# Attention decode step with a gated feed-forward on Trainium2: the first weight load as eight strided transfers

## The chip, the cores and the metric

The kernel runs on one core of a Trainium2 chip. A core has five engines that run their own instruction streams: TensorE (PE, matrix products), VectorE (DVE), ScalarE (ACT), GpSimd (POOL) and SyncE (SP). In this kernel SyncE issues all the transfers between HBM and the on-chip memory SBUF; the transfers themselves are carried out by 16 DMA engines, called movers below. SBUF has 128 partitions; a tile lies across partitions, and a row of a tile is what one partition holds of it.

The metric is the device time of one execution in microseconds (us). Before the change it is 696.29 us, the median of three runs (696.13 to 696.43).

## What is computed

Two branches read the same `x` of shape (2, 1, 640) and are mixed by a gate. Branch A is one decode step of attention with 32 heads over a cache of 4096 keys and values for each of 2 batch rows; branch B is a feed-forward layer with SiLU. All data are float32.

```python
g = sigmoid((x * gate_w).sum(-1, keepdims=True))

q = (x @ wq).reshape(B, Sq, 32, 128).transpose(0, 2, 1, 3)
scores = einsum("bhqd,bhkd->bhqk", q, k_cache) * 128 ** -0.5
o = einsum("bhqk,bhkd->bhqd", softmax(scores), v_cache)
a = o.transpose(0, 2, 1, 3).reshape(B, Sq, 4096) @ wo

b = einsum("bsf,fd->bsd", silu(einsum("bsd,df->bsf", x, w1)), w2)

return g * a + (1 - g) * b
```

The caches are most of the data: `k_cache` and `v_cache` have 134 MB each, `wq` and `wo` 10.5 MB each, `w1` (640 x 1728) and `w2` 4.4 MB each.

## The kernel before

**Tiles.** SBUF holds three large slabs, `a`, `b` and `v`, each 128 partitions of 16384 floats (64 KB a partition, 8.4 MB in all). The attention is cut into 16 items, a group of four heads of one batch row each. The K of an item fills slab `a` or `b` in turn, its V slab `v`. Each item's K is multiplied by the query and summed by VectorE (L666, L676) and GpSimd (L660), ScalarE takes the exponentials (L705), and TensorE multiplies by V (L756).

**The opening.** Before the first K the slabs serve for the weights. `w1`, viewed as 128 rows of 5 x 1728 floats (34,560 bytes a row), goes to columns 4096 to 12735 of slab `v`; `x` and the gate's weights go behind it in the same slab, on partitions 0 to 2. Of `wq`, four fifths go to slab `a` and the last fifth to the first 4096 columns of slab `v`; `w2` goes to slab `b`. SyncE issues these in the order w1, x, gate, wq (slab a), wq (slab v), w2, and none of them waits for another. TensorE then transposes x (L411), forms the gate (L433), multiplies x by wq (L458), spreads the first query (L478), rearranges the queries (L507) and multiplies x by w1 (L527). The feed-forward's second product with w2 is L584. K of item 0 goes to slab `a` after L458 has read wq there, V of item 0 to slab `v` after L527 has read w1.

**The close.** When the last item's V is in line, `wo` follows in seven transfers, the last three of them to slab `b`, and the output product (L607, L624, L637) adds both branches up.

**How the order is made.** The class `Flow` records every operation in program order, with the names that it reads and writes. `Flow.dma` (its issue shows as L68) gives every load its own semaphore; the 16 movers raise it by 16 in all when the load is complete. Names such as `v.3` stand for parts of a slab, and `part("v", 1, 2, 3, 4, 5)` lists the ones that w1 covers. `Flow.plan` goes through the operations and decides what each one waits for: it looks at the operations that it depends on, in a sorted order, and leaves out those that an earlier wait of the same engine already covers. `Flow.run` then writes the instructions, each behind its waits. The short first parts of the streams of ScalarE, VectorE and TensorE are written inside a small loop (`detour`), and TensorE's work for items 0 to 14 is a loop (`repeat`).

Of the kernel before, what the change touches and what calls it, by code (L numbers as in the profile page):

```python
# [16 lines left out]
class Flow:  # L17
# [22 lines left out]
    def op(self, eng, fn, reads=(), writes=(), by=(), signal=None, loop=None, after=(), lower=()):  # L40
        deps = list(after)
        for r in reads:
            if r in self.writer:
                deps.append(self.writer[r])
            if r.startswith("ps_"):
                deps += [d for d in self.readers.get(r, ()) if d.eng != eng]
        for w in writes:
            if w in self.writer:
                deps.append(self.writer[w])
            deps += self.readers.get(w, ())  # L50
        o = Op(eng, fn, deps, by, signal, loop)
        o.dma, o.lower = False, lower
        o.idx = len(self.ops[eng])
        self.ops[eng].append(o)
        self.all.append(o)
        for r in reads:
            self.readers.setdefault(r, []).append(o)
        for w in writes:
            self.writer[w], self.readers[w] = o, []
        return o  # L60
# [2 lines left out]

        return [self.writer[k] for k in keys if k in self.writer] + [o for k in keys for o in self.readers.get(k, ())]

    def dma(self, eng, dst, src, reads=(), writes=(), signal=None, after=()):
        e = self.engines[eng]
        o = self.op(eng, lambda: e.dma_start(dst, src), reads, writes, signal=signal, after=after)  # L68
        o.dma = True
        if signal is None:  # L70
            o.sem = self.sem(f"load_{len(self.all)}")
        return o

    def plan(self):
        seen = {e: {} for e in self.engines}
        for o in self.all:
            know = seen[o.eng]

            def done(d):
                return d in know.get("dma", ()) if d.dma else know.get(d.eng, -1) >= d.idx  # L80

            def learn(d):
                for e, v in d.know.items():
                    if e == "dma":
                        know["dma"] = know.get("dma", frozenset()) | v
                    else:
                        know[e] = max(know.get(e, -1), v)
                if d.dma:
                    know["dma"] = know.get("dma", frozenset()) | {d}
                else:  # L90
                    know[d.eng] = max(know.get(d.eng, -1), d.idx)

            for d in o.by:
                learn(d)
            for d in sorted(o.deps, key=lambda d: -d.idx):
                if (d.eng == o.eng == "PE") or done(d):
                    continue
                assert d.signal is None and o.loop is None, (o.eng, o.idx, d.eng, d.idx)
                o.waits.append(d)
                d.post = True  # L100
                learn(d)
            o.know = dict(know)
        for e, ops in self.ops.items():
            n = 0
            for o in ops:
                o.post = o.post or o.loop is not None
            for o in ops:
                n += o.post and not o.dma
                o.at = n

    def run(self, eng, ops=None):
        e = self.engines[eng]
        for o in self.ops[eng] if ops is None else ops:
            best = {}
            for d in o.waits:
                s, v = (d.sem, 16) if d.dma else (self.own[d.eng], d.at)
                best[s.name] = (s, max(v, best.get(s.name, (s, 0))[1]))
            for s, v in best.values():
                e.wait_ge(s, v)
            self.issue(o)  # L120
# [44 lines left out]
def gated_decode(nc, x, kc, vc, wq, wo, w1, w2, gate, out):  # L165
# [3 lines left out]
    F = w1.shape[1]  # L169
    J = D // P  # L170
    Q = 4
    QP = P // Q
    HQ = H // Q
    C = Q * SK // P
    NG = C // 4
# [10 lines left out]
    W2 = D // 2  # L186
    NP = HQ // 2
    PR = 2 * Q
    FIRST = 5
    LEAD = HB // 2  # L190
    PACED = (NP - 2) * PR
    items = [(hq, b) for hq in range(HQ) for b in range(B)]
    N = len(items)
# [3 lines left out]
    f = Flow(nc)  # L197
    V, S_, T_, G_ = nc.vector, nc.scalar, nc.tensor, nc.gpsimd

    def sb(name, shape, align=32):  # L200
        return nc.alloc_sbuf_tensor(name, shape, F32, align_bytes=align)[tuple([slice(None)] * len(shape))]

    def bank(name):
        return nc.alloc_psum_tensor(name, [P, 512], F32)[:, :]
# [3 lines left out]
    slab = {n: sb(f"slab_{n}", [P, SLAB], 512) for n in "abv"}  # L208

    def part(n, *ks):  # L210
        return [f"{n}.{k}" for k in (ks or range(8))]
# [11 lines left out]
    xz = sb("xz", [P, J, 32])  # L223
# [10 lines left out]
    spaced = sb("spaced", [P, FR, 32])  # L234
    qall = sb("qall", [P, HQ, B, DH])
    qsb = sb("qsb", [P, DH])
# [11 lines left out]
    ps_q, ps_o, ps_v, ps_acc, ps_t, ps_m, ps_0, ps_1 = (bank(f"ps{i}") for i in range(8))  # L248
# [8 lines left out]
    W1_AT = (J - J0) * H * DH  # L257
# [31 lines left out]
    def load_wo(g):  # L289
# [9 lines left out]


    wq_rows = wq.rearrange("(p j) n -> p (j n)", j=J)
    f.dma(
        "SP",
        slab["v"][:, W1_AT : W1_AT + J * F],
        w1.rearrange("(p j) f -> p (j f)", j=J),
        writes=part("v", 1, 2, 3, 4, 5),
    )
    xg = slab["v"][: B + 1, XG_AT : XG_AT + D]
    f.dma("SP", xg[:B], x.rearrange("b s d -> (b s) d"), writes=part("v", 6))
    f.dma("SP", xg[B : B + 1], gate[None, :], writes=part("v", 7))  # L310
# [6 lines left out]
        writes=part("b"),  # L317
# [8 lines left out]
        reads=["ident"],  # L326
        writes=["ident"],
# [8 lines left out]
    for q in range(Q):  # L336
        f.op(
            "DVE",
            lambda q=q: V.memset(fold[q * QP : (q + 1) * QP, :, q, :], 1.0),
            writes=["fold"] if q == 0 else [f"fold{q}"],  # L340
# [5 lines left out]
        reads=["ident"],  # L346
        writes=["sel"],
# [4 lines left out]
        reads=["ident"],  # L352
        writes=["half"],
# [9 lines left out]
        reads=["sel"],  # L363
        writes=["pick"],
# [4 lines left out]
        reads=["sel"],  # L369
        writes=["own"],  # L370
# [4 lines left out]
        reads=["ident"],  # L375
        writes=["side"],
    )
    for q in range(Q):
        f.op(
            "DVE",  # L380
            lambda q=q: V.tensor_copy(
                spread[:, q * QP : (q + 1) * QP], ident[:, 32 * q : 32 * q + 1].to_broadcast([P, QP])
            ),
            reads=["ident"],
            writes=[f"spread{q}"],
# [3 lines left out]
    for e in range(2):  # L389
# [6 lines left out]
            reads=["ident", "join"],  # L396
            writes=["join"],
        )
        for t in (at, at + 32):
# [3 lines left out]
                reads=["ident", "join"],  # L403
                writes=["join"],
# [18 lines left out]
    for b in range(B):  # L423
# [3 lines left out]
            reads=["ps_v", "xz"],  # L427
            writes=[f"gx{b}"],
# [5 lines left out]
        reads=["ones", "gp"],  # L434
        writes=["ps_o"],
# [7 lines left out]
        reads=["g"],  # L443
        writes=["gc"],
# [4 lines left out]
    qr = (ps_0, ps_1)  # L449
    HALF = HQ // 2  # L450

# [52 lines left out]
    for u in range(2):  # L504
# [9 lines left out]
            reads=["ident", f"qall{u}0"],  # L514
            writes=[f"ps_{u}"],
# [17 lines left out]
                )  # L533
        return last

    f.op("PE", mm_hr, reads=part("v", 1, 2, 3, 4, 5) + ["xz"], writes=["ps_v"])


    tv = turned[:, : 32 * FR].rearrange("p (n r) -> p n r", r=32)
# [2 lines left out]
    for e in range(2):  # L542
# [3 lines left out]
            reads=["ps_v"],  # L546
            writes=[f"spaced{e}"],
# [8 lines left out]
        reads=["he", "gc"],  # L556
        writes=["he"],
    )
    for e in range(2):
# [5 lines left out]
            reads=["he", "turned", "half", "seq"],  # L565
            writes=[f"seq{e}"],
# [132 lines left out]
    def weights(i):  # L699
        s = Ss[i % 2]  # L700

        def fn():
            for q in range(Q):
                lo, hi = q * QP, (q + 1) * QP
                last = S_.activation(  # L705
# [137 lines left out]
    for i in range(N + 1):  # L843
        j = i - 1
# [99 lines left out]
```

## Time and profile before

| | before |
|---|---|
| median of 3 runs | 696.29 us |
| lowest and highest | 696.13, 696.43 us |
| the profiled execution | 696.27 us |
| its span, first to last instruction | 694.9 us |
| bytes moved | 298.36 MB |
| mean rate over the span | 429 GB/s |
| VectorE, GpSimd, TensorE busy | 70%, 38%, 31% |

The span is cut into 40 equal slices, and a line of digits gives the busy share of each in tenths (9 is 90% or more); the line GB/s gives what the movers moved in each slice. In lists of instructions the first two numbers are the start and the duration in us; SPq marks SyncE's issuing of a transfer, which takes SyncE a few tenths of a microsecond, while the movement itself follows later. The list of issues gives the size of one transfer in KB of 1024 bytes and the time from issue to landing. In a table by stretches, each row has the stretch, its length, the busy time of PE, PE's weight load, DVE, ACT and POOL with the instructions in brackets, the granted TensorE clock, the busy share of the movers (over 1 where packets are counted to the stretch in which they begin) and GB/s.

### The profile page before, as it was taken

How to read it: one execution, taken by the hardware profiler on the slowest of the kernel's cores; microseconds unless marked ns; L12 is line 12 of the kernel's file. 1: busy time of each engine (PE TensorE's matmuls, PEld its weight loads, DVE VectorE, ACT ScalarE, POOL GpSimd, SP SyncE). 2: the span in 40 equal slices, each digit the busy share in tenths (PEclk: the TensorE clock that was granted, in tenths of full speed). 3: DMA queues.
4: the chain of work that ended last, by engine and by line, in shares of the span. 5: the costliest groups of instructions: out<-in, count | busy, mean ns of one | idle time of the engine just before them, and what ended most of it. 6: DMA issues, size and time to landing. Idle time of an engine off the chain costs nothing. (4 is left out here: it accounts for less than half of the span.)

```text
span 694.9 us, 3683 instructions
## 1 busy us (share of the span) xinstructions
PE 214.9 (31%) x1478; PEld 72.9 (10%) x1478; DVE 488.9 (70%) x263; ACT 41.2 (6%) x153; POOL 266.0 (38%) x26
## 2 busy tenths in 40 slices
PE   1085031151321406050412305060503215060557
PEld 1022010010110101010100101020101001020113
DVE  2001958898989596896959595986959595978901
ACT  0010010101010102010010101010000101010100
POOL 1000808191826090815335170906244260908100
PEclk9998557566665757575575757575665757575779
DMA  9999999999999999999999999999999999999997
GB/s 378 426 439 460 430 427 426 422 464 430 426 430 422 464 430 426 430 422 464 426 430 430 422 453 438 430 430 422 449 441 430 426 426 438 449 430 426 430 415 312
DMA packets 6217, 298.36 MB, mean 429 GB/s; under 512 B 695, under 2 KB 703, under 8 KB 962
## 3 DMA queue, kind: packets, MB, share of 16 engines
q1 hardware_dynamic: 6210, 298.27, 99.2%
q8 instruction: 4, 0.07, 0.0%
q14 instruction: 3, 0.02, 0.0%
HBM read 298.26 MB, written 0.01 MB: 429 GB/s over the span
## 5 line engine op out<-in xcount | busy, mean ns | idle before, releaser
L756 PE MATMUL ps<-slab_v,pz 128*32 128x512 f32 x960 | 134.7, 724 | 336.3 <-PEq L151 336.3
L660 POOL TENSOR_TENSOR slab_a<-slab_a,qsb 128x7680 f32<-128x7680 f32 x8 | 131.5, 16438 | 207.1 <-DMA slab_a<-in_A_k_cache_dram 192.0
L660 POOL TENSOR_TENSOR slab_b<-slab_b,qsb 128x7680 f32<-128x7680 f32 x8 | 131.4, 16424 | 171.5 <-DMA slab_b<-in_A_k_cache_dram 155.5
L676 DVE TENSOR_REDUCE s<-slab_a 128x68 f32<-128x8704 f32 (+1 forms) x16 | 138.2, 8676 | 0.0
L676 DVE TENSOR_REDUCE s<-slab_b 128x68 f32<-128x8704 f32 (+1 forms) x16 | 138.2, 8676 | 0.0
L666 DVE TENSOR_TENSOR slab_b<-slab_b,ps 128x8704 f32<-128x8704 f32 x8 | 73.7, 9218 | 48.9 <-DMA slab_b<-in_A_k_cache_dram 37.6
L666 DVE TENSOR_TENSOR slab_a<-slab_a,ps 128x8704 f32<-128x8704 f32 x8 | 73.7, 9219 | 45.3 <-DMA slab_a<-in_A_k_cache_dram 45.3
L756 PEld LDWEIGHTS ps<-slab_v,pz 128*32 128x32 f32 x960 | 37.0, 130 | 421.6 <-issue 421.6
L705 ACT ACTIVATE pz<-s,nb 32x128 f32<-32x128 f32 x64 | 25.5, 398 | 563.8 <-PE ps L756 390.7
L794 PE MATMUL ps<-osb,pick 128*128 128x512 f32 x32 | 20.4, 724 | 62.8 <-PEq L151 61.8
L778 DVE SCALAR_TENSOR_TENSOR osb<-ps,rg,own 128x512 f32<-128x512 f32 x16 | 12.0, 749 | 22.8 <-PE ps L756 22.4
L808 DVE TENSOR_REDUCE row<-ps 64x128 f32<-64x512 f32 x16 | 10.9, 682 | 23.3 <-PE ps L794 23.3
L545 DVE COPY spaced<-ps 128x224 f32<-128x224 f32 x2 | 0.7, 386 | 32.3 <-PE ps L527 32.3
L478 PE MATMUL ps<-qall,spread 128*128 (+1 forms) x32 | 7.4, 319 | 32.6 <-PEq L151 31.9
L458 PE MATMUL ps<-slab_a,xz 128*32 128x512 f32 x64 | 8.5, 690 | 16.2 <-DMA slab_a<-in_A_wq_dram 16.2
L794 PEld LDWEIGHTS ps<-osb,pick 128*128 128x128 f32 x32 | 5.4, 210 | 76.9 <-issue 75.0
L705 ACT ACTIVATION_READ_ACCUMULATOR pz<-s,nb 32x1 f32 x64 | 11.8, 184 | 0.0
L756 PE MATMUL ps<-slab_a,pz 128*32 128x512 f32 x64 | 9.3, 744 | 8.0 <-DMA slab_a<-in_A_v_cache_dram 8.0
L478 PEld LDWEIGHTS ps<-qall,spread 128*128 128x128 f32 x32 | 6.6, 224 | 42.8 <-issue 41.2
L815 DVE STREAM_TRANSPOSE ps<-row 64x256 f32<-64x256 f32 x16 | 10.3, 643 | 0.6
L584 PE MATMUL ps<-slab_b,seq 128*32 128x320 f32 x54 | 9.4, 506 | 3.0 <-DVE seq L562 3.0
L607 PE MATMUL ps<-slab_v,oP 128*32 128x320 f32 x96 | 9.2, 434 | 0.6 <-DMA slab_v<-in_A_wo_dram 0.5
(70 smaller groups left out, 92.1 us busy)
## 6 DMA issues: line engine op xcount, KB each, us to landing
slab_v<-in_A_wo_dram SPq DMA_DIRECT2D x2, 2560.0 KB, 19.4
slab_v<-in_B_w_dram SPq DMA_DIRECT2D x1, 4320.0 KB, 14.1
slab_b<-in_B_w_dram SPq DMA_DIRECT2D x1, 4320.0 KB, 46.4
slab_v<-in_A_wo_dram SPq DMA_DIRECT2D x2, 1280.0 KB, 26.7
slab_v<-in_A_wq_dram SPq DMA_DIRECT2D x1, 2048.0 KB, 36.7
slab_b<-in_A_wo_dram SPq DMA_DIRECT2D x1, 1600.0 KB, 31.2
slab_b<-in_A_wo_dram SPq DMA_DIRECT2D x1, 640.0 KB, 32.3
slab_b<-in_A_wo_dram SPq DMA_DIRECT2D x1, 320.0 KB, 32.6
```

The lines of the kernel that those rows point to most:

```text
L478: return T_.matmul(ps_q[:, :DH], spread, qall.rearrange("p h b d -> p (h b) d")[:, i, :], start=True, stop=True,)
L584: last = T_.matmul(early[to : to + 32, :], seq[:, k : k + 2, :].rearrange("p k z -> p (k z)"), slab[n][:, k * HD : (k + 1) * HD], start=(k ...
L607: last = T_.matmul(early[to + 32 * n : to + 32 * n + 32, :], oP[:, at : at + 32], slab["v"][:, s_ * D + n * W2 : s_ * D + (n + 1) * W2], s ...
L660: lambda: G_.tensor_mul(k[:, CV:, :], k[:, CV:, :], qsb[:, None, :].to_broadcast([P, C - CV, DH])),
L666: lambda: V.tensor_mul(k[:, :CV, :], k[:, :CV, :], ps_q[:, None, :DH].to_broadcast([P, CV, DH])),
L676: lambda c0=c0, c1=c1: V.reduce_sum(Ss[i % 2][:, c0:c1], k[:, c0:c1, :], axis=AX.X),
L705: last = S_.activation(pz[lo:hi, :, 4 * q : 4 * q + 4], s[lo:hi].rearrange("p (g c) -> p g c", c=4), AF.Exp, bias=nb[lo:hi], scale=SCALE, ...
L756: last = T_.matmul(ps_v[32 * q : 32 * q + 32, :], pz[:, gr, :], v[:, gr, :], start=(gr < 4), stop=(gr >= NG - 4),)
L778: lambda: V.scalar_tensor_tensor(osb, ps_v.rearrange("p (c d) -> p c d", d=DH), rg, own[:, :, None].to_broadcast([P, 4, DH]), op0=ALU.mult ...
L794: lambda *_: T_.matmul(ps_o, pick, osb.rearrange("p c d -> p (c d)"), start=True, stop=True),
L808: lambda: V.reduce_sum(row, ps_o[:64].rearrange("p (c d) -> p d c", d=DH), axis=AX.X),
L815: lambda: V.transpose(oT.rearrange("p n (e i) -> p n e i", e=2), twice),
```

## The change

The w1 load becomes eight loads. Load `r` takes the rows r, r + 8, ..., r + 120 of the view of 128 rows, whole rows of 34,560 bytes, and puts them on the partitions of the same numbers. All eight raise one semaphore, `load_w1`, and the reader, L527, waits for it to reach 16 x 8 = 128. `Flow.dma` gets two arguments for this, the semaphore and the full count, and `Flow.run` waits for that count. The parts `v.1` to `v.5` are no longer named as written by w1; names `w1.0` to `w1.7` stand in their place, and L527 reads both sets. `Flow.plan` sorts the dependences by the place in the whole program (`turn`) instead of the place in their engine's stream (`idx`).

```diff
@@ class Flow
         o.idx = len(self.ops[eng])
+        o.turn = len(self.all)
...
-    def dma(self, eng, dst, src, reads=(), writes=(), signal=None, after=()):
+    def dma(self, eng, dst, src, reads=(), writes=(), signal=None, after=(), sem=None, full=16):
...
         if signal is None:
-            o.sem = self.sem(f"load_{len(self.all)}")
+            o.sem = sem or self.sem(f"load_{len(self.all)}")
+        o.full = full
...
-            for d in sorted(o.deps, key=lambda d: -d.idx):
+            for d in sorted(o.deps, key=lambda d: -d.turn):
...
-                s, v = (d.sem, 16) if d.dma else (self.own[d.eng], d.at)
+                s, v = (d.sem, d.full) if d.dma else (self.own[d.eng], d.at)
@@ gated_decode
+    EACH = 8
...
-    f.dma(
-        "SP",
-        slab["v"][:, W1_AT : W1_AT + J * F],
-        w1.rearrange("(p j) f -> p (j f)", j=J),
-        writes=part("v", 1, 2, 3, 4, 5),
-    )
+    w1_to, w1_from = slab["v"][:, W1_AT : W1_AT + J * F], w1.rearrange("(p j) f -> p (j f)", j=J)
+    h_w1 = f.sem("load_w1")
+    for r in range(EACH):
+        f.dma("SP", w1_to[r::EACH], w1_from[r::EACH], writes=[f"w1.{r}"], sem=h_w1, full=16 * EACH)
...
-    f.op("PE", mm_hr, reads=part("v", 1, 2, 3, 4, 5) + ["xz"], writes=["ps_v"])
+    f.op("PE", mm_hr, reads=part("v", 1, 2, 3, 4, 5) + [f"w1.{r}" for r in range(EACH)] + ["xz"], writes=["ps_v"])
```

In the order of the instructions, SyncE's stream has eight issues of 16 rows in place of the one of 128 rows, ahead of x; fifteen of VectorE's products on K (L666) lose their wait for TensorE and keep those for ScalarE and for the load; the first K issue loses its wait for wq's load and keeps that for TensorE. The other engines' orders are the same. The new `dma` arguments move the line numbers by one or two (L68 is L69, L411 is L412, L458 is L459, L527 is L528).

## The prediction

> **What bounds the kernel now.** I read the page's head first, then the row of its 40 slices and its queue rows.
>
> ```profile
> span 694.9 us, 3683 instructions
> PE 214.9 (31%) x1478; PEld 72.9 (10%) x1478; DVE 488.9 (70%) x263; ACT 41.2 (6%) x153; POOL 266.0 (38%) x26
> ...
> DMA  9999999999999999999999999999999999999997
> GB/s 378 426 439 460 430 427 426 422 464 430 426 430 422 464 430 426 430 422 464 426 430 430 422 453 438 430 430 422 449 441 430 426 426 438 449 430 426 430 415 312
> DMA packets 6217, 298.36 MB, mean 429 GB/s; under 512 B 695, under 2 KB 703, under 8 KB 962
> ...
> q1 hardware_dynamic: 6210, 298.27, 99.2%
> ```
>
> No compute engine is above 70%; the transfers are above 90% in 39 of 40 slices. The rate has no dip after the first slice, so the question is whether the stream ever stands still. A table by stretches of the inner part, and the chain of waits, answer it.
>
> ```profile
> core 0: us, PE busy (x) PEld busy (x) DVE busy (x) ACT busy (x) POOL busy (x), PEclk, DMA share, GB/s
> 17.40:677.60 660.20, 199.16 (x1298) 64.82 (x1298) 483.13 (x231) 39.53 (x151) 262.89 (x16) 0.66 1.00 434
> ```
>
> ```profile
> 656.93 0.33 SPq L68
> ...
> 658.73 31.24 DMA slab_b<-in_A_wo_dram
> 689.97 0.14 issue
> 690.10 2.69 PE ps L637 x64
> ```
>
> From 17.4 to 677.6 us the 16 movers are busy for 1.00 of the time at 434 GB/s, and the chain ends on the last wo transfer, issued 31 us before it lands: it was in line behind others all that time. So the end is the start of the stream, plus 298.27 MB at its rate, plus a tail of some 5 us. A delay of the whole stream at the front comes out one for one at the end, if nothing later runs dry. The front is this (SyncE's issues and the first users on TensorE, from the timeline; the landing of the first weights from the page's list of issues):
>
> ```profile
> 0.74 0.39 SPq L68 DMA_DIRECT2D slab_v<-in_B_w_dram  x1
> 1.19 0.33 SPq L68 DMA_DIRECT2D slab_v<-in_A_x_dram  x1
> 1.57 0.23 SPq L68 DMA_DIRECT2D slab_v<-in_gate_w_dram  x1
> 1.84 0.36 SPq L68 DMA_DIRECT2D slab_a<-in_A_wq_dram  x1
> ...
> 2.77 0.44 SPq L68 DMA_DIRECT2D slab_b<-in_B_w_dram  x1
> ```
>
> ```profile
> slab_v<-in_B_w_dram SPq DMA_DIRECT2D x1, 4320.0 KB, 14.1
> slab_b<-in_B_w_dram SPq DMA_DIRECT2D x1, 4320.0 KB, 46.4
> ```
>
> ```profile
> 14.26 2.33 PE L411 MATMUL ps<-ident,slab_v 3*128 3x3 f32 x10 [14.26 <-DMA slab_v<-in_A_x_dram]
> ...
> 34.16 8.47 PE L458 MATMUL ps<-slab_a,xz 128*32 128x512 f32 x64 [16.18 <-DMA slab_a<-in_A_wq_dram]
> ```
>
> ```profile
> 42.76 0.33 SPq L68 DMA_DIRECT2D slab_a<-in_A_k_cache_dram  x1
> 51.09 0.33 SPq L68 DMA_DIRECT2D slab_v<-in_A_v_cache_dram  x1
> ```
>
> The w1 transfer is issued at 0.74 and lands by 14.84. All six opening transfers are in line by 3.2 us, the last of them (w2) lands at 2.77 + 46.4 = 49.2, and the next one (K of the first item) joins at 42.8: 6.4 us before the line would be empty. That is the smallest margin of the front, and it moves with the stream, since the K issue waits for the product on wq, which itself waits for wq's landing.
>
> **The change part by part.** *Issues.* One w1 issue becomes eight, seven more on SyncE. From one issue's start to the next takes 0.27 to 0.45 us in the rows above, so x, gate, wq and w2 are issued about 7 x 0.45 = 3.2 us later, wq at 5.0 instead of 1.84. The cover is w1's own movement: wq is needed in line only when w1's last rows have gone, past 13 us. One eighth is 0.553 MB, 1.27 us at 434 GB/s, so issues at 0.45 us stay ahead of the movers. Without that cover it would cost the 3.2 us. Cost taken: nothing.
>
> *Completion marks.* The page's 695 packets under 512 B are 16 for each of the 43 transfers over 128 partitions, and 7 for x, gate and the output. Seven more transfers would make 807, and 6322 packets on q1. What a boundary between small transfers costs is seen at the end, where the last wo block goes out in three pieces (issues from the timeline; landings from the list of issues):
>
> ```profile
> 658.73 1.38 SPq L68 DMA_DIRECT2D slab_b<-in_A_wo_dram  x3
> ```
>
> ```profile
> slab_b<-in_A_wo_dram SPq DMA_DIRECT2D x1, 1600.0 KB, 31.2
> slab_b<-in_A_wo_dram SPq DMA_DIRECT2D x1, 640.0 KB, 32.3
> slab_b<-in_A_wo_dram SPq DMA_DIRECT2D x1, 320.0 KB, 32.6
> ```
>
> Three issues in 1.38 us start about 0.47 apart, so the second piece lands 0.47 + 1.1 = 1.57 us after the first and the third 0.47 + 0.3 = 0.77 after the second. At 434 GB/s their bytes alone take 1.51 and 0.76. A boundary costs 0.01 to 0.06 us, seven of them at most 0.4; I take nothing.
>
> *Waits.* TensorE's w1 product (L527) waits for one semaphore at 128 instead of 16. It stands behind the wq product that ran from 34.16 on, 19 us after w1 is there; a w1 that takes twice as long is still hidden. The new sort key of the planner drops a wait for TensorE from 15 of VectorE's key products (L666) and a wait for wq's load from the first K issue; each keeps a wait that comes later anyway (ScalarE's copy of the same query; the product that read wq), so nothing moves. With both I take nothing.
>
> *The front end of the stream.* In half-microsecond stretches of the start:
>
> ```profile
> 1.00:1.50 0.50, 0.00 (x0) 0.00 (x0) 0.00 (x0) 0.00 (x0) 0.30 (x2) 1.00 0.00 0
> 1.50:2.00 0.50, 0.00 (x0) 0.00 (x0) 0.00 (x0) 0.26 (x1) 0.50 (x2) 1.00 2.80 691
> 2.00:2.50 0.50, 0.00 (x0) 0.00 (x0) 0.33 (x3) 0.50 (x1) 0.50 (x2) 1.00 0.89 276
> 2.50:3.00 0.50, 0.00 (x0) 0.00 (x0) 0.36 (x5) 0.50 (x1) 0.50 (x2) 1.00 0.38 138
> 3.00:3.50 0.50, 0.00 (x0) 0.00 (x0) 0.50 (x3) 0.02 (x1) 0.50 (x2) 1.00 0.00 0
> 3.50:4.00 0.50, 0.00 (x0) 0.00 (x0) 0.47 (x5) 0.00 (x0) 0.37 (x1) 1.00 0.97 415
> ```
>
> Packets are counted where they begin, so the first ones begin between 1.5 and 3.0 us, most of them before 2.5, and the next ones near 4.0. A w1 row is 34,560 B; at 434/16 = 27.1 GB/s it takes 1.27 us, so the first row of an early mover takes 0.7 to 0.8 us more than it needs. A first transfer of 16 rows instead of 128 may be set up sooner. It can't begin before its issue has ended, at 1.13: the gain lies between 0 and 0.9 us. I take 0.4, the middle, since no row says when in that gap the set-up ends.
>
> *The pattern of partitions.* This carries the forecast. Before, each transfer of this size covers all 128 partitions; after, the rows in flight at one time are sixteen partitions eight apart, r, r+8, ..., r+120, the same r on all movers. No row of this trace shows a large transfer to fewer than 128 partitions. What the rows do show is a ceiling: 434 GB/s with all movers at 1.00, for wq, K, V and wo alike, thus a limit at the movers or at their ways into SBUF. If the limit is the movers, each has one row and loses nothing: 0 us. If it is the ways, and these are dealt out by low digits of the partition number, a common step of eight sends several rows of one transfer the same way while other ways idle, and the smallest such crowding, two rows for a way, halves the rate: w1 takes 2 x 10.2 (4.424 MB at 434 GB/s) instead of 10.2 us, **+10.2**. Four to a way would be +30.6. Between 0 and 10.2 I take the upper end: every row at the ceiling had whole tiles, none supports that a sixteenth of the partitions, taken at a power-of-two step, still reaches it.
>
> [...]
>
> A little of the doubling is hidden. Now w1's last row lands at 14.84, while x, which is in line behind w1 rows of its own movers, has been read from 14.26 on: movers are some 0.6 us apart. Where two share a way, one that is late leaves it to its partner. I take -0.5.
>
> Sum: 10.2 - 0.5 - 0.4 = 9.3 on the profiled execution's 696.27 (694.9 of span and 1.4 around it; the median is 696.29): **705.6 us**.
>
> **The rivals.**
> *Movers are the limit; nothing is lost.* For it: each transfer still gives each of the 16 movers one whole row, the same bytes. Against it: only the argument above. The gain at the front less the marks, +0.4 to -0.9: 695.4 to 696.7, I say 696.0.
> *Faster.* The front gives all that its stretches allow: 0.9 us for the set-up and the 0.6 us by which movers are apart, since the movers start level: 694.8. For it: the end waits for the last mover. Against it: the first rows already begin within 1.5 us of each other, and what makes a mover late is not shown to be the set-up.
> *Each transfer pays its start in series.* The eight run down one after the other; the 0.8 us that the first row loses at the start is paid seven more times, 696.3 + 5.6 = 701.9. It decides once the movers don't overlap one transfer's end with the next one's start. Against it: the 0.01 to 0.06 us at the wo pieces. [...]
> *Crowding that is half hidden.* The movers of a crowded pair drift apart and use different ways in turn, 696.3 + 5 = 701.3. [...] Against it: all movers begin within about 1.5 us.
> *It does not do what it says.* Sixteen rows fall on fewer than 16 movers, several in a row: then marks are fewer than 807, and with different movers taken by different transfers the time is that of the first rival; its chance is in there.
>
> **How the numbers follow.** Two rows to a way: 0.61, own range 704.3 to 706.8 (skew and front at their bounds, marks 0.4). Half hidden crowding 0.06, starts in series 0.03, fourfold crowding (about 726) 0.01: slower in all, 0.71. Nothing lost 0.24. Faster by more than 0.2% 0.05. I count 0.2%, 1.4 us, as what a measurement can tell from no change. The range, 695.3 to 707.0, takes in all of the likeliest case and the one in which nothing is lost.
>
> **What would show it.** In the page of the changed kernel: under 512 B 807, if all movers take part. The first of the 40 slices falls from 378 to near 190 GB/s if two rows share a way (217 GB/s from about 2.2 us on, over 17.6 us), and stays at 378 or a little more if not. x's matmul (L412 there) starts near 24 instead of 14.26, the wq product near 43 instead of 34.16, the inner rate stays at 434. The forecast is wrong if the first slice holds its rate; if the slice falls and the end does not follow, a later margin took it. If the wq product comes at 38 to 40, it is a start per transfer or a half hidden crowding: with starts in series there are stretches with no packet between the eighths.

## The result and the profile after

The changed kernel takes 707.15 us (median of 5 runs, 707.09 to 707.39); the kernel before, beside it, 696.29 us. The ratio is 1.0156, with a 95% interval of 1.0145 to 1.0167: 10.86 us slower. The prediction said slower, 705.6 us, and a range up to 707.0; the measured time lies 0.15 us above that range.

The head, the slices and the packet counts of the changed kernel's page:

```profile
span 706.0 us, 3689 instructions
...
DMA  9999999999999999999999999999999999999997
GB/s 200 350 424 454 442 416 443 442 420 427 457 423 420 460 427 416 453 438 416 453 434 420 427 457 423 423 460 423 416 460 431 416 453 438 416 434 449 423 414 305
DMA packets 6329, 298.36 MB, mean 423 GB/s; under 512 B 807, under 2 KB 815, under 8 KB 1074
...
q1 hardware_dynamic: 6322, 298.27, 99.2%
```

The bytes are the same and the line of busy digits is that of before, yet the first slice has 200 GB/s instead of 378 and the second 350 instead of 426; from the third on the numbers lie around those of before. So the loss enters while w1 moves, and nothing later takes it back. Here the first slice's busy digit is 9 at 200 GB/s as at 378: it does not tell a mover that works from one that is held up; only the GB/s line shows it. There are 807 small packets, 112 more, so each of the eight transfers has 16 completion marks: all movers take part.

The stretch from 4 to 22 us, all of it w1, from the table by stretches of the changed kernel:

```profile
4.00:22.00 18.00, 0.00 (x0) 0.00 (x0) 1.42 (x12) 0.00 (x0) 0.00 (x0) 1.00 1.01 212
```

212 GB/s is 0.49 of the 434 GB/s of the inner part before. The front in the timeline of the changed kernel, first SyncE's issues, then TensorE's first users:

```profile
0.74 6.58 SPq L69 DMA_DIRECT2D slab_v<-in_B_w_dram  x8
7.36 0.48 SPq L69 DMA_DIRECT2D slab_v<-in_A_x_dram  x1
7.90 0.23 SPq L69 DMA_DIRECT2D slab_v<-in_gate_w_dram  x1
8.17 0.36 SPq L69 DMA_DIRECT2D slab_a<-in_A_wq_dram  x1
```

```profile
24.85 2.33 PE L412 MATMUL ps<-ident,slab_v 3*128 3x3 f32 x10 [24.85 <-DMA slab_v<-in_gate_w_dram]
27.91 0.59 PE L434 MATMUL ps<-gp,ones 128*128 128x2 f32 x2 [0.73 <-DVE gp L431]
44.56 1.93 PE L459 MATMUL ps<-slab_a,xz 128*32 128x512 f32 x8 [16.06 <-DMA slab_a<-in_A_wq_dram]
```

x's product starts at 24.85 instead of 14.26, the wq product at 44.56 instead of 34.16: 10.6 and 10.4 later. The eight issues take 6.58 us together, 0.82 on the average and not 0.45 (seven take 0.57 to 0.75 each, one 1.98), and wq is issued at 8.17; that is still hidden, since w1's last rows begin at 22.2.

### The profile page after: what moved, and what is told of

It is laid out like the page before. It is cut to its first block, busy times and chain, and to the rows that moved or that the text cites. A ratio compares the mean times of both kernels' runs of the same rounds, so it can differ in the third digit from the quotient of the medians.

```text
span 706.0 us, 3689 instructions
## 1 busy us (share of the span) xinstructions
PE 216.7 (31%) x1478; PEld 73.1 (10%) x1478; DVE 488.8 (69%) x263; ACT 41.2 (6%) x153; POOL 266.1 (38%) x26
## 5 line engine op out<-in xcount | busy, mean ns | idle before, releaser
L757 PE MATMUL ps<-slab_v,pz 128*32 128x512 f32 x960 | 137.0, 735 | 335.9 <-PEq L153 335.9
L459 PE MATMUL ps<-slab_a,xz 128*32 128x512 f32 x64 | 8.6, 697 | 16.1 <-DMA slab_a<-in_A_wq_dram 16.1
```

The source lines that it names most:

```text
L459: last = T_.matmul(qr[u][32 * q : 32 * q + 32, :], xz[:, j, :], w[:, u * HALF : (u + 1) * HALF, q, :], start=(j == 0), stop=(j == J - 1),)
L757: last = T_.matmul(ps_v[32 * q : 32 * q + 32, :], pz[:, gr, :], v[:, gr, :], start=(gr < 4), stop=(gr >= NG - 4),)
```

## The experiments

Each experiment is an edit of the changed kernel, and is compared with the kernel before in runs on the same chip (696.29 to 696.40 us there). The theory: what limits a transfer is the way into SBUF, and sixteen partitions eight apart meet two to a way. Code cuts are shortened: `...` stands for arguments that stay.

**One transfer again.** `EACH = 1`; the new planner order and the shared semaphore stay.

```diff
-    EACH = 8
+    EACH = 1
```

> The changed kernel with one w1 transfer of all 128 partitions again; the new planner order, the dropped waits and the shared-semaphore code stay. Theory (rows of one transfer crowd on the ways into SBUF): the whole loss goes, 696.3 us, within 0.3. Rival (the planner's new order or the shorter instruction streams cost the part that the doubled w1 stage does not explain): 696.7 to 697.5.

Measured 696.45 us, ratio 1.0001 (0.9991 to 1.0011). The planner's new order and the dropped waits cost nothing; all of the loss belongs to how w1 is cut.

**Eight transfers, cut by columns.**

```diff
-        f.dma("SP", w1_to[r::EACH], w1_from[r::EACH], ...)
+        c0, c1 = r * J * F // EACH, (r + 1) * J * F // EACH
+        f.dma("SP", w1_to[:, c0:c1], w1_from[:, c0:c1], ...)
```

> Eight w1 transfers as in the change, the same bytes in each, but cut by columns: each covers all 128 partitions with 1080 floats a row. Theory (crowding): every transfer reaches all ways, so no loss beyond seven boundaries of at most 0.06 us and rows of 4,320 B: 696.0 to 697.0 us, first slice of the page near 378 GB/s. Rival (starts in series, a cost per transfer): the same loss as the change, 702 to 707 us.

Measured 697.11 us, ratio 1.0016 (1.0001 to 1.0030), against 707.15 with the same number of transfers of the same size. The number of transfers and their size are not the cause; start-ups in series would have shown here. The 0.7 us is a little more than the expected range's end (the ten runs lie between 696.57 and 697.24, but for one of 701.72). In the trace one mover lands the first K 1.9 us behind all others, while the average of the 16 is 0.34 later than before; what holds that one was not followed.

**Sixteen neighbouring partitions.**

```diff
-        f.dma("SP", w1_to[r::EACH], w1_from[r::EACH], ...)
+        p0, p1 = r * P // EACH, (r + 1) * P // EACH
+        f.dma("SP", w1_to[p0:p1], w1_from[p0:p1], ...)
```

> Eight w1 transfers of sixteen neighbouring partitions each (0 to 15, 16 to 31, ...), neither side strided. [...] Rivals: the step of eight is what hurts (HBM side or partition side): 696.3; the number of small transfers is what hurts: 707.

Measured 722.54 us, ratio 1.0372 (1.0355 to 1.0389). Slower by far than the change, so neither the step of eight nor the number of transfers is what hurts; the step of eight even helps. It is less than the 726 or so that the prediction gives for fourfold crowding, though. The stretch from 4 to 34 us of this kernel:

```profile
4.00:34.00 30.00, 0.00 (x0) 0.00 (x0) 1.41 (x12) 0.00 (x0) 0.00 (x0) 1.00 1.03 121
```

121 GB/s where fourfold crowding would leave 434 / 4 = 108: 3.6 times slower than the full rate, not 4.

**Two halves of 64 partitions.**

```diff
-    EACH = 8
+    EACH = 2
...
+        p0, p1 = r * P // EACH, (r + 1) * P // EACH
+        f.dma("SP", w1_to[p0:p1], w1_from[p0:p1], ...)
```

> Two w1 transfers of 64 neighbouring partitions each (0 to 63, 64 to 127). Theory (crowding): 64 neighbours reach half of the ways, two rows in flight to a way: w1 takes 20.4 us, 706 to 707.5 us. Rival (only transfers of sixteen rows, one row for each mover, are slow): 696.3.

Measured 707.51 us, ratio 1.0158 (1.0141 to 1.0175): two large transfers lose as much as eight small ones, when each covers only half of the partitions in one piece. Its rate from 4 to 22 us:

```profile
4.00:22.00 18.00, 0.00 (x0) 0.00 (x0) 1.41 (x12) 0.00 (x0) 0.00 (x0) 1.00 1.04 215
```

**HBM side or SBUF side.** In both pairs so far the source moved with the destination. Two kernels cross them.

```diff
-        f.dma("SP", w1_to[r::EACH], w1_from[r::EACH], ...)
+        p0, p1 = r * P // EACH, (r + 1) * P // EACH
+        f.dma("SP", w1_to[r::EACH], w1_from[p0:p1], ...)
```

> Destination as in the change (sixteen partitions eight apart), source sixteen neighbouring rows of w1 in HBM, so the rows of w1 land permuted and the feed-forward branch is computed with permuted weights. Theory (crowding on the SBUF side): as the change, 706.5 to 707.7 us. Rival (the HBM side of sixteen neighbouring rows is what made the neighbouring-rows kernel slower still): 722.

```diff
-        f.dma("SP", w1_to[r::EACH], w1_from[r::EACH], ...)
+        p0, p1 = r * P // EACH, (r + 1) * P // EACH
+        f.dma("SP", w1_to[p0:p1], w1_from[r::EACH], ...)
```

> The other way round: source sixteen rows eight apart in HBM as in the change, destination sixteen neighbouring partitions; again the rows of w1 land permuted. Theory (SBUF side): as the kernel of neighbouring rows, 721.5 to 723.5 us. Rival (HBM side): 707.

Measured 706.60 us (ratio 1.0148, 1.0128 to 1.0168) for the strided destination and 722.72 us (1.0379, 1.0359 to 1.0400) for the neighbouring one. Their rates while w1 moves, in the same order:

```profile
4.00:22.00 18.00, 0.00 (x0) 0.00 (x0) 1.41 (x12) 0.00 (x0) 0.00 (x0) 1.00 1.01 210
```

```profile
4.00:34.00 30.00, 0.00 (x0) 0.00 (x0) 1.42 (x12) 0.00 (x0) 0.00 (x0) 1.00 1.02 122
```

The time follows the destination's partitions, whatever the source. The limit lies on the SBUF side.

**Larger strided transfers.** `EACH = 4` (32 partitions four apart) and `EACH = 2` (64 partitions two apart), nothing else.

> Four transfers of 32 partitions four apart. [...] Theory A (rows dealt to the movers in order, so that the rows in flight at one time still meet two to a way): 707 us. Theory B (the dealing of a larger transfer follows the ways): 696.3 us.

> Two transfers of 64 partitions two apart. Theory A (dealt in order): 707 us. Theory B (dealt by the ways as soon as there are enough rows): 696.3 us. A value between, 699 to 704, would say that the movers drift apart and use different ways part of the time.

Measured 696.28 us (ratio 0.9999, 0.9989 to 1.0009) and 696.23 us (0.9999, 0.9989 to 1.0009): no loss in either. The stretch from 4 to 13 us, and the packets, of the kernel with four transfers:

```profile
4.00:13.00 9.00, 0.00 (x0) 0.00 (x0) 1.40 (x12) 0.00 (x0) 0.00 (x0) 1.00 1.01 434
```

```profile
DMA packets 6265, 298.36 MB, mean 429 GB/s; under 512 B 743, under 2 KB 751, under 8 KB 1010
```

743 is 48 more than 695, 16 marks for each of three further transfers: all movers have a part of each. Theory A, dealing in order, would leave two rows in flight to a way in both kernels and falls. Nor do the movers share ways part of the time: in the packet records of both kernels the w1 rows after each mover's first two took 1.28 to 1.30 us, where most of the changed kernel's took 2.67. So the rows of these two kernels did not crowd; by what rule they are dealt was not measured. A strided transfer as such cost nothing here.

**Half the dose.**

```diff
+    HALF_W = J * F // 2
+    f.dma("SP", w1_to[:, :HALF_W], w1_from[:, :HALF_W], writes=["w1.whole"])
     for r in range(EACH):
-        f.dma("SP", w1_to[r::EACH], w1_from[r::EACH], ...)
+        f.dma("SP", w1_to[r::EACH, HALF_W:], w1_from[r::EACH, HALF_W:], ...)
...
-    f.op("PE", mm_hr, reads=part("v", 1, 2, 3, 4, 5) + [f"w1.{r}" ...
+    f.op("PE", mm_hr, reads=part("v", 1, 2, 3, 4, 5) + ["w1.whole"] + [f"w1.{r}" ...
```

> Half of w1's columns go out first in one transfer of all 128 partitions, the other half in the eight transfers of sixteen partitions eight apart (rows of 17,280 B). Theory (crowding lengthens each strided row by the same factor, seen as 2.67 us instead of 1.28 for a whole row): the crowded half takes 10.6 instead of 5.1 us, 696.3 + 5.5 = 701.8 us, up to 702.9 where the later instruction fetch meets the last mover. Rival (a fixed cost of the eight strided transfers, whatever their size): 706 to 707.

Measured 702.51 us, ratio 1.0090 (1.0073 to 1.0107): +6.2 for half of the bytes, against +10.86 for all. The loss goes mainly with the bytes that are crowded, and a fixed cost of the eight strided transfers, whatever their size, falls as the main cause. It is 0.8 us more than half of 10.86, though, so a part does not shrink with the bytes. Such a part is seen at the change from w1 to wq: by the trace's packets the first row of wq takes 3.60 us there, on the average of the movers, instead of 2.42 before.

No version beat the kernel before: the two with 32 and 64 strided partitions to a transfer are its equals.

## Why the prediction was right and where it was wrong

**What bounds the kernel: right.** The stream of transfers never stands still, and a delay at its front came out at the end. GpSimd starts its part of the first two K as they land; the kernel before, then the changed one, from the timelines:

```profile
68.50 16.44 POOL L660 TENSOR_TENSOR slab_a<-slab_a,qsb 128x7680 f32<-128x7680 f32 x1 [64.62 <-DMA slab_a<-in_A_k_cache_dram]
107.41 16.40 POOL L660 TENSOR_TENSOR slab_b<-slab_b,qsb 128x7680 f32<-128x7680 f32 x1 [22.48 <-DMA slab_b<-in_A_k_cache_dram]
```

```profile
78.98 16.40 POOL L661 TENSOR_TENSOR slab_a<-slab_a,qsb 128x7680 f32<-128x7680 f32 x1 [75.11 <-DMA slab_a<-in_A_k_cache_dram]
118.96 16.43 POOL L661 TENSOR_TENSOR slab_b<-slab_b,qsb 128x7680 f32<-128x7680 f32 x1 [23.57 <-DMA slab_b<-in_A_k_cache_dram]
```

The first K is 10.48 us late, the second 11.55, the end of the span 11.1.

**Issues, marks, waits at nothing: right,** but for the first issue. The eight took 6.6 us instead of about 3.6, and seven of them are still under cover; the first is not, as the front shows below. The rival of start-ups in series fell with the column cut, the rival of half hidden crowding with the steady 212 GB/s.

**The pattern of partitions: right in mechanism and nearly in size.** The two values between which the prediction chose, 0 and 10.2, are both near what was found: 32 and 64 strided partitions cost nothing, and sixteen lengthened w1's own rows by 9.7 us (below). That two rows meet on a way, and not four, no row of the trace before showed; by the rows the prediction took the smallest crowding, and there it was lucky too: sixteen neighbours cost 26 us. That the ways are dealt out by low digits of the partition number was the author's assumption. The runs show that the rate goes with the destination's partitions (212 GB/s for sixteen partitions eight apart, 121 for sixteen neighbours, 215 for 64 neighbours, 434 for 32 four apart), and not which partitions share a way.

**The step that failed is the two deductions, -0.4 for the front and -0.5 for the movers' distance, and a loss at the change from w1 to wq that has no term.** The front: the changed kernel's first packets, in half-microsecond stretches,

```profile
1.50:2.00 0.50, 0.00 (x0) 0.00 (x0) 0.00 (x0) 0.26 (x1) 0.50 (x2) 1.00 0.06 16
2.00:2.50 0.50, 0.00 (x0) 0.00 (x0) 0.32 (x3) 0.50 (x1) 0.50 (x2) 1.00 3.76 862
```

begin after 2.0 us, where before they had begun between 1.5 and 2.0 (691 GB/s in that row): later, not sooner. The first strided issue took 0.61 us instead of 0.39, and the first row of w1 began at 2.13 instead of 1.75. The start of the wq product says the same: it was to come near 43, and came at 44.56, so the forecast was short before any K had moved.

The trace has a record of each packet, without the mover's name, and of the time at which each of the 16 movers raised the semaphore of a load. Averages over the 16 movers, in us on the clock of the timelines:

| | before | changed | more |
|---|---|---|---|
| first row of w1 begins | 2.03 | 2.54 | 0.51 |
| the eight rows of w1 take | 11.07 | 20.76 | 9.69 |
| first row of wq begins | 13.20 | 23.39 | 10.19 |
| first row of wq takes | 2.42 | 3.17 | 0.75 |
| second row of wq begins | 15.61 | 26.56 | 10.95 |

So the front was +0.5 instead of -0.4. The crowding was 9.7, a little under the 10.2: most rows of w1 took 2.67 us where they had taken 1.28, but each mover's first row had been slow before too (2.03 us on the average, then 2.38). And the first rows of wq, which begin while other movers still have rows of w1, took 0.75 longer, for which the prediction has no term. Together that is 10.95, where the prediction had 10.2 - 0.4 = 9.8.

The movers' distance: the prediction took it as 0.6 us from x's product, while the landings of w1 before lie between 13.19 and 14.81. The landings of later loads by mover ("strided dest." is the kernel with the strided destination and the neighbouring source):

```
load                       average   first mover  last but one   last
first K,  before             67.24         66.91         68.04   68.42
first K,  after              78.23         77.68         78.75   78.84
first K,  strided dest.      78.08         77.73         78.50   79.11
second K, before            105.97        105.51        107.08  107.27
second K, after             116.92        116.26        117.44  118.83
second K, strided dest.     116.77        116.33        117.71  117.96
last wo,  before            690.71        690.15        691.76  692.24
last wo,  after             701.63        700.90        702.75  703.32
last wo,  strided dest.     701.49        700.95        702.45  702.69
```

The average mover of the changed kernel is 10.99 late at the first K, 10.95 at the second and 10.92 at the last wo transfer: that loss enters once and stays. The last mover is 10.42 late at the first K, so 0.57 of the movers' distance was hidden there, near the 0.5 taken. But at the second K it is 11.56 late and at the last wo transfer 11.08, 0.16 more than the average: of what was hidden nothing was left at the end. That makes the 11.1 of the span (706.0 - 694.9); the medians differ by 10.86, the profiled execution of the changed kernel being the longest of its five.

What set the last mover back is argued, not shown. At the second K it falls 1.39 us behind the others. In the trace's packets a fetch of 16,384 B of instructions, 0.97 us long, begins at 114.5 us. The kernel before has the same fetch at 103.0 us (0.95 us), but its last mover took 38.85 us from the first K to the second, against 39.99. In the kernel with the strided destination, equally crowded, the last mover took 38.85 as well (79.11 to 117.96), and the time was 0.55 us less, 706.60. So the fetch would have met the last mover in the changed kernel and not in these two; no run took the fetch away.

**The chances.** The likeliest case came true, and its own range, 704.3 to 706.8, was too narrow by 0.35 us: its upper end took the front and the movers' distance to cost nothing at worst, and the front cost 0.5; the change to wq was not in it. Its lower end does not come out of the bounds that it names: 696.27 + 10.2 - 0.9 - 0.6 is 705.0.

## What to carry to other kernels

When a load is cut into pieces, cut the columns and keep all the partitions (0.7 us for eight pieces here), or keep strided pieces large: here 32 partitions four apart cost nothing, sixteen eight apart halved the rate (212 GB/s of 434), sixteen neighbours brought it to 0.28 (121). In a stream that never stands still, read the GB/s line and not the busy digits, and expect a loss at the front to come out whole at the end (10.95 us here when wq's second rows begin, 10.92 at the last wo transfer, for the average mover). Work out such a sum for the average mover, which shows what was lost, and for the last one, which sets each landing.

## What the runs showed of the hardware that was not expected

Sixteen neighbouring partitions moved 121 GB/s, and 122 with the source strided, more than the 108 of a rate cut to a quarter, while sixteen strided ones and 64 neighbours, at 210 to 215, lie just under half, 217. In the packet records of the sixteen neighbours the rows of one transfer begin over 2.5 us, and most take 4.69 us and not 4 x 1.28 = 5.12. In the changed kernel the rows of the fifth eighth took 2.48 us on the average, those of all others but the first 2.61 to 2.67. What makes these rows quicker, no run shows.

The time of SyncE's issues goes with the destination as well: eight transfers of sixteen strided partitions took 6.58 us, eight of sixteen neighbouring ones 3.68, and with the sides crossed it was 6.85 for the strided destination and 4.13 for the neighbouring one. But the two issues of 64 neighbouring partitions took 0.58 us each, as long as most strided ones, so it is not the step alone; what it is stays open.

```profile
0.74 3.68 SPq L69 DMA_DIRECT2D slab_v<-in_B_w_dram  x8
```
